# Three shared buffers between the copies of an accumulator and the transposes of u: who takes the third one, and three durations in the planner

## The chip, the cores and the metric

The kernel runs on one core of one Trainium2 chip. The metric is the device time of one execution in microseconds. The time before is 1109.25 us, the median of 3 runs (1109.18, 1109.25 and 1109.59 us). The execution that was profiled took 1109.22 us; its span, from the first to the last recorded instruction, is 1107.4 us, so 1.82 us of it lie around the span.

## The reference

Eight batches, each with a sequence of S = 3008 rows. An attention without softmax gates u, and an MLP mixer follows it, first over the tokens and then over the channels:

```python
def _attn_ref(u, v, z):                       # u, v: (8, 3008, 256), z: (8, 3008, 64)
    scores = (1.0 / S) * np.matmul(z, z.transpose(0, 2, 1))
    attn = np.maximum(scores, 0.0) ** 2
    return u * np.matmul(attn, v)

def _moe_ref(x, w_tok1, w_tok2, w_ch1, w_ch2):   # x is what the attention gave
    xt = x.transpose(0, 2, 1)
    h = np.maximum(xt @ w_tok1, 0.0) @ w_tok2     # 3008 -> 256 -> 3008
    u = x + h.transpose(0, 2, 1)
    h2 = np.maximum(u @ w_ch1, 0.0) @ w_ch2       # 256 -> 1536 -> 256
    return u + h2
```

## The kernel before, in words

**Tiling.** A batch `b` is cut into `NQ` = 6 blocks `q` of 512 rows (the last has 448). For each block the attention adds up `acc`, two accumulators `dh` = 0 and 1 of 128 columns of v each; each accumulator is held as two halves in a pair of PSUM banks, since the matmuls of `av_matmul` (L708) work on 64 rows at a time, two beside each other.

**From an accumulator to x.** When the last matmul of an accumulator is issued, `finish` (L820) plans three steps. `copy` (L833) has ACT copy one half to a buffer `cp` (L837); `add` (L842) has DVE add the other half to it (L843), after which the PSUM pair is free; `gate` (L854) has DVE multiply it with u (L865, and L870 for the 64 columns that are left in the last block) into `xT`, after which `cp` is free. After the second gate of a block, SP turns `xT` by a DMA transpose into `x_pair` (`turn_x`, L903), DVE makes differences of it (`x_sums`, L940), and from all six blocks `tok1` (L1075) begins the token mixer of the batch.

**The mixer.** `tok1` of six blocks gives `a_ps`. `collect_a` (L1095 on ACT, L1091 and L1106 on DVE) and `relu_a` (L1127 on ACT for one half, L1125 on DVE for the other) turn it into `a_f`; `tok2` (L1145) multiplies that and adds it to `xT` (L1154). From then on `xT` holds the mixer's u. `turn_u2` (L1176, DMA on SP at L1180) turns it into `u_sb`, which the output needs as the residual. The channel mixer is `ch1` (matmuls L1209 into `hp`, L1248 on ACT into `h2pre`) or, for some blocks, a form with fewer matmuls (`grouped_ch1`, L1340 into `gp`, with copies and activations at L1348, L1351, L1355 and L1359 on ACT). Then come seven `product`s per block (L1478, into `xb` and `zb`), from `h2pre` and from sums that DVE makes of it (`hsum`, L1414 to L1432). `collect` adds them, and `u_sb`, into `ro` (L1530, L1524); SP writes `ro` out (L1535).

**The three buffers.** `cp` and `u_sb` share one tag of three buffers (`tag="res", bufs=3`). A tile takes its buffer in the order in which the program is written down, and its first writer waits until what held the buffer is read.

**Who sets the order.** Nothing is ordered by hand and nothing at run time. While the program is built, a small simulation keeps a clock for PE (`pe[0]`), ACT, DVE and SP (`free`), and lists of waiting operations (`push`). `next_op` (L388) takes the operation that could start first: at the latest of its engine's time, its `ready`, and the first entry of its list `frees`, and only if its condition `room` holds. `push(engine, ready, busy, lat, fn)` states how long the engine is held and when the result is there. The work of PE is a list of `Piece`s with `needs`; `next_piece` (L1749) takes one whose needs are met at the clock's time, or within 0.05 us of it. `Sooner(done, us)` is a need that may be met `us` later than the piece's begin, because only a later matmul of the piece reads it. The instructions then stand in each engine's queue in the simulated order, and on the chip each queue works strictly in that order, waiting on semaphores where the data is not there.

**The stretches.** Attention and mixer alternate: when the last block of a batch is through its matmuls, `goal` is raised and only mixer pieces are taken: blocks q = 3, 4 and 5 of the batch before, then `tok1` and `tok2` of this batch, then its blocks 0 to 2. The transpose of u of blocks over `HALF` = 3 waits for that moment (L1168); that of block 3 is made at the end of the stretch before and holds one of the three buffers all through the attention.

**What the counters say before the change.** `copies[0]` counts copies between `copy` and `gate`, `live["us"]` the `u_sb` in use. A copy is planned only if `copies[0] + live["us"] < 3` (L850), a `turn_u2` if `live["us"] < 2` (L1167), whatever the copies hold. No time is kept at which a buffer comes free.

Of the kernel before, what the change touches and what calls it, by code (L numbers as in the profile page):

```python
# [69 lines left out]
def kernel(  # L70
# [298 lines left out]
    ROOM = {"at": 6, "fl": 11, "xT": 9, "h2": 6, "us": 2}  # L369
    at_free = [0.0] * ROOM["at"]  # L370
    fl_free = [0.0] * ROOM["fl"]
    ring = [(Done(0.0), i) for i in range(RING)]

    def first_acc(dh):
# [10 lines left out]
    def has_room(names):  # L385
        return names() if callable(names) else all(live[n] < ROOM[n] for n in names)
# [196 lines left out]
    def release(name, uses, t=0.0):  # L583
        uses[0] -= 1
        uses[1:] = [max([t] + uses[1:])]
        if not uses[0]:
            live[name] -= 1
            if name == "at":
                at_free.append(uses[1])
            if name == "fl":  # L590
                fl_free.append(uses[1])


    class Block:
# [225 lines left out]
    def finish(blk, dh, end):  # L820


        W, acc = blk.W, blk.acc[dh]
        summed = Done()
        guess[blk.home[dh]] = end + 1.7
        ring.append((summed, blk.home[dh]))

        def load(e):
            return max(free[e], end) + sum(op.busy for op in waiting[e])

        on_act = blk.b > 0 or load("act") + 0.46 < load("dve") + 0.67

        def copy(t):  # L833
            copies[0] += 1
            cp = sb.tile([P, QW], F32, tag="res", name="cp", bufs=3)
            if on_act:
                nc.scalar.copy(cp[:, :W], acc[:, 1, :W])  # L837
            else:
                nc.vector.tensor_copy(cp[:, :W], acc[:, 1, :W])
            push("dve", t, 0.66, 0.78, lambda t: add(cp, t), first=1, done=summed)  # L840

        def add(cp, t):  # L842
            nc.vector.tensor_add(cp[:, :W], acc[:, 0, :W], cp[:, :W])  # L843
            push("dve", t - 0.12, 0.58, 0.7, lambda t: gate(blk, dh, cp, t), first=1,
                 room=(lambda: (blk.b, blk.q) in uTs and has_room(("xT",))) if dh == 0
                 else lambda: (blk.b, blk.q) in xTs)

        engine, busy = ("act", 0.56 if blk.q == NQ - 1 else 0.46) if on_act else ("dve", 0.66)
        push(engine, end + 0.21, busy, busy + 0.15, copy, first=1,
             room=lambda: copies[0] + live["us"] < 3)  # L850

    gated, copies = [0], [0]

    def gate(blk, dh, acc, t):  # L854
        copies[0] -= not blk.whole
        b, q, W = blk.b, blk.q, blk.W
        uT = uTs[b, q]
        if dh == 0:
            xTs[b, q] = sb.tile([P, DT, QW], BF16, tag="xT", name="xT", bufs=ROOM["xT"])
            live["xT"] += 1  # L860
            if W < QW:
                nc.gpsimd.memset(xTs[b, q][:, :, W:], 0.0)
        xT = xTs[b, q]
        full, rest = W // P, W % P
        nc.vector.tensor_mul(  # L865
            xT[:, dh, :full * P].rearrange("p (t s) -> p t s", s=P),
            acc[:, :full * P].rearrange("p (t s) -> p t s", s=P),
            uT[:, :full, dh, :])
        if rest:
            nc.vector.tensor_mul(  # L870
                xT[:, dh, full * P:W], acc[:, full * P:W], uT[:, full, dh, :rest])
        if dh == DT - 1:
            if b == 0 and q > 1:
                release("fl", [1], t)
            gated[0] += 1
            push("sp", t, 1.25, 7.5 if q < NQ - 1 else 12.0, lambda t: turn_x(b, q, t),
                 first=1 if b == 0 or q >= NQ - 2 else -1,
                 room=x_room(b, q), frees=fl_free if b and q % 2 == 0 else ())
# [166 lines left out]
    def add_mixer(b):  # L1045
# [6 lines left out]
        def tok1(q, end):  # L1052
# [28 lines left out]
            if q == NQ - 1:  # L1081
                home = "fl" if b else "h2"

                def collect_a(t):
# [20 lines left out]
                    def one_high(t):  # L1105
                        nc.vector.tensor_add(f[:, 1, :], a_ps[:, 0, 3, :], f[:, 4, :])  # L1106
                        st["a"] = f[:, 6:8, :].rearrange("p k d -> p (k d)").bitcast(
                            BF16).rearrange("p (m d) -> p m d", m=2)
                        push("act", t, 0.3, 0.47, lambda t: relu_a(0, t), first=2,
                             done=a_done[0])  # L1110
                        push("dve", t - 0.16, 0.58, 0.72, both_high, first=2,
                             done=a_done[1])
# [26 lines left out]
        def tok2(q, end):  # L1139
# [9 lines left out]
            def add(t):  # L1149

                xT = xTs[b, q]
                n = full_tiles[q]
                to = xT[:, :, :n * P].rearrange("p h (t s) -> p h t s", t=n)
                nc.vector.tensor_add(  # L1154
                    to, to, h[:, :, :n * P].rearrange("p h (s t) -> p h t s", t=n))
                if n * P < W:
                    to = xT[:, :, n * P:W]
                    nc.vector.tensor_add(to, to, h[:, :, n * P:W])
                if W < QW and b % 2:

                    nc.gpsimd.tensor_copy(xT[:, :, W:], xT[:, :, W - TAIL:W])
                    t += 0.5
                u_done[q].t = t
                if ("want", q) in st:
                    st.pop(("want", q))(t)
                st["turned", q] = push("sp", t, 1.25, 5.5, lambda t: turn_u2(q, t), first=1,
                                       room=lambda: has_room(("us",)) and (  # L1167
                                           q <= HALF or goal[0] > (b, 1 + HALF)))  # L1168
            ring.append((push("dve", end + 0.21, 1.12, 1.25, add, first=2), slot))
            if q == NQ - 1:  # L1170
# [4 lines left out]

        def turn_u2(q, t):  # L1176
            live["us"] += 1
            turned_back[b] += 1
            us = sb.tile([P, DT, QW // P, P], BF16, tag="res", name="u_sb", bufs=3)
            nc.sync.dma_start_transpose(  # L1180
                out=us.rearrange("p h t d -> p (h t) d"),
                in_=xTs[b, q].rearrange("p h s -> p (h s)"))
            st["u", q] = us
            release("xT", xT_uses[q])
            for waits in st.pop(("waits", q), []):
                waits(t)
# [306 lines left out]
        def collect(q, k, end):  # L1493
# [24 lines left out]
            def add(t):  # L1518
# [15 lines left out]
                if not over[q]:  # L1534
# [1 line left out]
                        out=rows_of(out[b], q)[:, :2 * n, :], in_=st["res", q][:, :2 * n, :])  # L1536
                    free["sp"] = max(free["sp"], t) + 0.4
                    release(home_of(q), [1], t + 4.0)
                    release("us", us_uses[q])

            ready = end + 0.21
            done = taken[q, k]
# [41 lines left out]
        def ch2(q, half, i, end):  # L1584
# [23 lines left out]
            def residual(t):  # L1608
# [33 lines left out]
                        nc.sync.dma_start(out=to, in_=res[r, j, :])  # L1642
                free["sp"] = max(free["sp"], t) + 0.4
                if last:
                    release("us", us_uses[q])
            freed = Done()
            cost = 1.4 if both and b % 2 else 0.62
            with_u(q, end + 0.21, lambda at: push(
# [48 lines left out]

        def add_product(q, k):
            needs = {
                1: [Sooner(h2_done[q, c], 0.111 * c) for c in range(CHT // 2)] + w_done[2:],  # L1700
                2: [taken[q, 1]], 5: [mix_done], 6: [taken[q, 1]], 3: [taken[q, 5]], 7: [taken[q, 6]],
                4: [taken[q, 7]]}[k]
            if k == 2:
                needs = needs + [Read(taken[q, j]) for j in (6, 7)]
            kind = {5: 0, 7: 1, 6: 2, 4: 3}.get(k)
            if kind is not None:
                needs = needs + [Sooner(s_done[q, d, kind], 0.222 * d) for d in range(CHT // 4)]
            if q == NQ - 1 and k == 5 and b % 2 == 0:
                needs = needs + [tok1_over[b + 1]]
            cost = pairs_of(q) * (CHT // 2) * column_time(P)  # L1710
# [438 lines left out]
```

## Time and profile before

| | |
|---|---|
| median of 3 runs | 1109.25 us (1109.18 to 1109.59) |
| the profiled execution | 1109.22 us |
| its span | 1107.4 us |
| PE busy in the span | 1102.1 us, 11235 matmuls |
| DVE, ACT, POOL busy | 816.0, 694.9, 168.3 us |

PE is TensorE, DVE VectorE, ACT ScalarE, POOL GpSimd and SP SyncE. The chain of waits is the profile's account of what ended last, followed back step by step. In a timeline each row has its start and its length in us, the engine, the line of the kernel, the operation, what it writes and reads, the shape, and how many equal instructions are merged in it; in brackets stands how long the engine had nothing to do just before, and what ended that. Matmuls overlap in the pipeline, so the pace of PE is read from start to start: a 128x512 matmul takes 0.216 us that way, although its row shows a longer time. A wait inside a run of matmuls shows only there.

### The profile page before, as it was taken

Reading aid. Unit: us, or ns where it says so; the run is one execution under the profiler, and the core shown is the slowest. Engines: PE = TensorE matmul, PEld = TensorE weight load, DVE = VectorE, ACT = ScalarE, POOL = GpSimd, SP = SyncE. Lnnn points to the kernel's source line nnn. Section 1 sums busy time; section 2 is a strip of 40 time slices with the busy share of each in tenths; the row PEclk is TensorE's granted clock in tenths of the full one; section 3 lists DMA queues with packets and bytes.
Section 4 is the critical chain, followed back from the end, with each engine's and each line's share of the span. In section 5 each row is a group of like instructions: output and inputs, shape, how many; then the busy total and the mean of one; then the engine's idle time right before and its main releaser. Section 6 shows DMA issues by size and latency. Waiting matters only on the chain.

```text
span 1107.4 us, 27564 instructions
## 1 busy us (share of the span) xinstructions
PE 1102.1 (100%) x11235; PEld 699.6 (63%) x11235; DVE 816.0 (74%) x1727; ACT 694.9 (63%) x965; POOL 168.3 (15%) x386
## 2 busy tenths in 40 slices
PE   9999999999999999999999999999999999999998
PEld 3445575677557665576655865557655677556776
DVE  6889865877758867578765787667866778656785
ACT  8999565646855567556675467654766637753474
POOL 5320110321002110032100311003110030000100
PEclk9999999999999999999999999999999999999999
DMA  9999948797979979789697896976988769595213
GB/s 178 164 190 181 165 96 152 124 177 149 184 122 157 170 143 185 127 155 195 130 175 121 157 195 147 186 131 126 197 159 169 139 122 203 118 158 106 71 59 96
DMA packets 465728, 165.58 MB, mean 150 GB/s; under 512 B 433024, under 2 KB 448960, under 8 KB 465600
## 3 DMA queue, kind: packets, MB, share of 16 engines
q1 hardware_dynamic: 436208, 131.11, 59.0%
q0 software_dynamic: 28880, 32.32, 21.4%
q8 instruction: 88, 1.44, 0.6%
q14 instruction: 40, 0.33, 0.1%
q10 hardware_dynamic: 512, 0.38, 0.1%
HBM read 65.40 MB, written 24.64 MB: 81 GB/s over the span
## 4 chain that ended last, share of the span: by engine, by line
PE 97%; DVE 2%; ACT 1%; DMA 0%; issue 0%; POOL 0%; ACTq 0%
PE acc L708 41%; PE hp L1209 17%; PE xb L1478 13%; PE sc L481 6%; PE zb L1478 5%; PE gp L1340 4%; PE h_ps L1145 4%; PE a_ps L1075 3%; PE op L1599 2%; PE first_acc L625 1%; DVE at L527 1%; DMA v_sb<-in_v_dram 0%; ACT h2pre L1248 0%; PE wp L221 0%; DVE cp L843 0%; DVE shared_sb L985 0%
## 5 line engine op out<-in xcount | busy, mean ns | idle before, releaser
L708 PEld LDWEIGHTS <-v_sb 64*128 64x128 bf16 x4418 | 246.3, 94 | 211.5 <-issue 0.6
L708 PE MATMUL acc<-at,v_sb 64*128 64x512 bf16 (+1 forms) x2738 | 342.0, 375 | 0.0
L519 ACT ACTIVATE at<-sc 128x1024 bf16<-128x1024 f32 (+1 forms) x290 | 287.5, 1027 | 75.5 <-PE sc L481 70.0
L1248 ACT ACTIVATE h2pre<-hp 128x1024 bf16<-128x1024 f32 (+1 forms) x227 | 222.7, 1004 | 166.9 <-PE hp L1209 165.4
L527 DVE TENSOR_TENSOR at<-at 128x1024 bf16<-128x1024 bf16 (+1 forms) x290 | 197.0, 687 | 112.7 <-ACT at L519 107.6
L1209 PE MATMUL hp<-xT,w_ch_sb 128*128 128x512 bf16 (+1 forms) x936 | 227.2, 374 | 0.0
L708 PE MATMUL acc<-fl,v_sb 64*128 64x512 bf16 (+1 forms) x1680 | 192.9, 367 | 0.0
L1478 PEld LDWEIGHTS <-hsum 128*128 128x128 bf16 x2088 | 127.7, 98 | 12.1 <-issue 1.7
L481 PE MATMUL sc<-zT 64*128 64x512 bf16 (+1 forms) x732 | 133.2, 359 | 0.2 <-ACT zT L1977 0.2
L1209 PEld LDWEIGHTS <-w_ch_sb 128*128 128x128 bf16 x936 | 86.0, 98 | 72.2 <-issue 0.8
L1478 PEld LDWEIGHTS <-h2pre 128*128 128x128 bf16 x1566 | 96.6, 98 | 12.3 <-ACT h2pre L1248 0.4
L837 ACT COPY cp<-acc 128x512 f32<-128x512 f32 (+1 forms) x94 | 55.0, 585 | 76.8 <-PE acc L708 65.4
L843 DVE TENSOR_TENSOR cp<-acc,cp 128x512 f32<-128x512 f32 (+1 forms) x94 | 63.4, 674 | 47.7 <-ACT cp L837 47.3
L1414 DVE TENSOR_TENSOR hsum<-h2pre 128x1024 bf16<-128x1024 bf16 (+1 forms) x141 | 89.9, 649 | 10.5 <-ACT h2pre L1248 8.4
L1478 PE MATMUL xb<-w_ch_sb,h2pre 128*128 128x128 bf16 x1044 | 74.3, 219 | 0.2 <-ACT h2pre L1248 0.2
L140 POOL CAST mark<-at 128x1 f32<-128x1 bf16 x29 | 11.7, 403 | 411.0 <-DVE at L527 411.0
L1478 PE MATMUL xb<-shared_sb,hsum 128*128 128x128 bf16 x1044 | 73.7, 219 | 0.0
L507 ACT ACTIVATE at<-sc 128x512 bf16<-128x512 f32 (+3 forms) x152 | 56.0, 449 | 27.6 <-PE sc L481 23.3
L481 PEld LDWEIGHTS <-zT 64*128 64x128 bf16 x732 | 42.7, 94 | 41.4 <-issue 4.4
L865 DVE TENSOR_TENSOR xT<-cp,uT 128x512 bf16<-128x512 f32 (+1 forms) x94 | 62.9, 669 | 3.1
L1154 DVE TENSOR_TENSOR xT<-xT,h_ps 128x1024 bf16<-128x1024 bf16 (+1 forms) x48 | 55.6, 1172 | 3.1 <-PE h_ps L1145 2.8
L1432 DVE TENSOR_TENSOR hsum<-h2pre,hsum 128x512 bf16<-128x512 bf16 (+1 forms) x141 | 55.2, 401 | 2.3
(116 smaller groups left out, 1130.1 us busy)
## 6 DMA issues: line engine op xcount, KB each, us to landing
out_dram<-ro SPq DMA_DIRECT2D x40, 512.0 KB, 2.9
v_sb<-in_v_dram POOLq DMA_DIRECT2D x40, 256.0 KB, 4.6
ur<-in_u_dram POOLq DMA_DIRECT2D x40, 256.0 KB, 5.4
w_tok_sb<-in_moe_w_tok_dram POOLq DMA_DIRECT2D x10, 256.0 KB, 10.7
shared_sb<-in_z_dram POOLq DMA_DIRECT2D x35, 64.0 KB, 4.2
at<-at SPq DMA_TRANSPOSE x114, 2.4
out_dram<-ro SPq DMA_DIRECT2D x7, 256.0 KB, 3.7
fl<-at SPq DMA_TRANSPOSE x105, 4.5
```

The source lines that it names most:

```text
L481: nc.tensor.matmul(sc[:, r, c0:c1], zT[h, k:k + P], zT[h, m + c0:m + c1], start=True, stop=True)
L507: nc.scalar.activation(a3[:, i, c0:c1], sc[:, r, c0:c1], ACT.Relu, scale=inv_S)
L519: nc.scalar.activation(view, sv, ACT.Relu, scale=inv_S)
L527: nc.vector.tensor_mul(view, view, view)
L708: nc.tensor.matmul(o, vs[blk.b, g][rows, i, dh * P:(dh + 1) * P], rhs, start=(dh, h) not in blk.begun, stop=stop, skip_group_check=True)
L843: nc.vector.tensor_add(cp[:, :W], acc[:, 0, :W], cp[:, :W])
L865: nc.vector.tensor_mul(xT[:, dh, :full * P].rearrange("p (t s) -> p t s", s=P), acc[:, :full * P].rearrange("p (t s) -> p t s", s=P), uT[: ...
L1154: nc.vector.tensor_add(to, to, h[:, :, :n * P].rearrange("p h (s t) -> p h t s", t=n))
L1209: nc.tensor.matmul(hps[r % len(hps)][:, r, :W], w_ch1_sb[:, dc, cc * P:(cc + 1) * P], xT[:, dc, :W], start=(dc == 0), stop=(dc == DT - 1))
L1248: nc.scalar.activation(h2[:, :, :W], hp[:, :, :W], ACT.Relu)
L1414: nc.vector.tensor_sub(sums["s"][:, 0:2, :, :n * P], h[:, :, 1], h[:, 0])
L1478: nc.tensor.matmul(to[:, i * P:(i + 1) * P], lhs, weights[:, c2, :], start=(first_use and c2 == 0 and i == 0), stop=(c2 == CHT // 2 - 1), ...
```

## The change

Four things are edited.

1. A list `res_free` keeps the times at which the three `res` buffers come free, as the simulation has them. A copy and a `turn_u2` each take an entry; `gate` and the last use of `u_sb` each put one back. The copy is pushed with `frees=res_free`, so that it is planned no sooner than a buffer is free.
2. `turn_u2` also needs `copies[0] + live["us"] < 3`, and that `closing[0]` does not hold. `closing[0]` is set when an accumulator of the last block of a batch (from batch 1 on) is through its matmuls, and cleared when the copy of the second accumulator has its buffer.
3. `relu_a` of the first half on ACT is planned with 0.42 us held and 0.57 us to its result, instead of 0.3 and 0.47.
4. The allowances of `add_product` depend on how many pairs of 128 columns the block has (`pairs_of(q)`: 2, and 1 for the last block): 0.0556 us for each matmul instead of 0.111 us for each two, and 0.111 instead of 0.222. For the blocks with two they stay 0.111 and 0.222; for the last block they are halved.

```diff
     fl_free = [0.0] * ROOM["fl"]
+    res_free = [0.0] * 3
...
             if name == "fl":
                 fl_free.append(uses[1])
+            if name == "us":
+                res_free.append(uses[1])
...
         ring.append((summed, blk.home[dh]))
+        closing[0] = blk.b > 0 and blk.q == NQ - 1
...
         def copy(t):
             copies[0] += 1
+            res_free.pop(0)
+            if dh == DT - 1:
+                closing[0] = False
             cp = sb.tile([P, QW], F32, tag="res", name="cp", bufs=3)
...
         push(engine, end + 0.21, busy, busy + 0.15, copy, first=1,
-             room=lambda: copies[0] + live["us"] < 3)
-    gated, copies = [0], [0]
+             room=lambda: copies[0] + live["us"] < 3, frees=res_free)
+    gated, copies, closing = [0], [0], [False]
     def gate(blk, dh, acc, t):
-        copies[0] -= not blk.whole
+        if not blk.whole:
+            copies[0] -= 1
+            res_free.append(t)
...
-                        push("act", t, 0.3, 0.47, lambda t: relu_a(0, t), first=2,
+                        push("act", t, 0.42, 0.57, lambda t: relu_a(0, t), first=2,
                              done=a_done[0])
...
                 st["turned", q] = push("sp", t, 1.25, 5.5, lambda t: turn_u2(q, t), first=1,
                                        room=lambda: has_room(("us",)) and (
+                                           copies[0] + live["us"] < 3 and not closing[0]) and (
                                            q <= HALF or goal[0] > (b, 1 + HALF)))
...
         def turn_u2(q, t):
             live["us"] += 1
+            res_free.pop(0)
...
-                    release("us", us_uses[q])
+                    release("us", us_uses[q], t)
...
-                1: [Sooner(h2_done[q, c], 0.111 * c) for c in range(CHT // 2)] + w_done[2:],
+                1: [Sooner(h2_done[q, c], 0.0556 * pairs_of(q) * c) for c in range(CHT // 2)] + w_done[2:],
...
-                needs = needs + [Sooner(s_done[q, d, kind], 0.222 * d) for d in range(CHT // 4)]
+                needs = needs + [Sooner(s_done[q, d, kind], 0.111 * pairs_of(q) * d) for d in range(CHT // 4)]
```

More of the change, by code (lines that the diff above doesn't have):

```diff
@@ L1644, in residual @@
                 if last:
-                    release("us", us_uses[q])
+                    release("us", us_uses[q], t)
             freed = Done()
```

## Prediction

> **What bounds the kernel now.** First the page: span, busy times, and the shares of the chain that ended last.
>
> ```profile
> span 1107.4 us, 27564 instructions
> ...
> PE 1102.1 (100%) x11235; PEld 699.6 (63%) x11235; DVE 816.0 (74%) x1727; ACT 694.9 (63%) x965; POOL 168.3 (15%) x386
> ...
> PE 97%; DVE 2%; ACT 1%; DMA 0%; issue 0%; POOL 0%; ACTq 0%
> ```
>
> PE bounds the kernel, and the change removes none of its matmuls. It can only win or lose moments in which PE waits, and these are small: the 3% of the chain that is not PE's hold the start, the tail and every stall. Next, the table of waits, for the wait that the change names:
>
> ```profile
> ACT cp L837 <- DVE xT L870: 10.5, 6, 1.8
> ```
>
> Six times ACT stands before a copy until the gate of an earlier copy is through, 10.5 us in all. These are the ends of batches, L870 being the last block's second part. Timelines of SP, DVE and ACT there, batch 5:
>
> ```profile
> 742.76 1.30 SPq L1180 DMA_TRANSPOSE u_sb<-xT  x1
> ...
> 744.51 0.22 DVE L870 TENSOR_TENSOR xT<-cp,uT 128x64 bf16<-128x64 f32 x1
> ...
> 744.82 0.53 ACT L837 COPY cp<-acc 128x448 f32<-128x448 f32 x1 [1.80 <-DVE xT L870]
> ...
> 745.38 0.62 DVE L843 TENSOR_TENSOR cp<-acc,cp 128x448 f32<-128x448 f32 x1 [0.32 <-ACT cp L837]
> ...
> 746.80 1.23 SPq L903 DMA_TRANSPOSE x_pair<-xT  x1
> ```
>
> Block 3's u and the first copy hold two buffers; the transpose of block 4's u takes the third; so the second copy waits until the first is gated (744.73) and starts at 744.82. Its sum, which frees the PSUM pair, ends at 746.00. PE in the same stretch:
>
> ```profile
> 743.90 0.39 PE L1340 MATMUL gp<-xT,w_ch_sb 128*128 128x256 bf16 x2
> ...
> 745.01 1.03 PE L1209 MATMUL hp<-xT,w_ch_sb 128*128 128x512 bf16 x4
> 746.06 0.83 PE L1478 MATMUL zb<-shared_sb,hsum 128*128 128x128 bf16 x12
> ...
> 748.80 0.38 PE L1340 MATMUL gp<-xT,shared_sb 128*128 128x256 bf16 x2
> ```
>
> Attention is done at 743.90. From the four `hp` matmuls to the next run 1.05 us pass; the next run begins 0.06 us after that sum. Whether this is a loss is told by the last batch, where the same pieces run:
>
> ```profile
> 1012.72 0.39 PE L1340 MATMUL gp<-xT,w_ch_sb 128*128 128x256 bf16 x2
> ...
> 1013.31 0.53 ACT L837 COPY cp<-acc 128x448 f32<-128x448 f32 x1 [1.47 <-DVE xT L870]
> ...
> 1013.83 1.03 PE L1209 MATMUL hp<-xT,w_ch_sb 128*128 128x512 bf16 x4
> 1014.70 0.83 PE L1478 MATMUL zb<-shared_sb,hsum 128*128 128x128 bf16 x12
> 1015.37 0.38 PE L1340 MATMUL gp<-xT,w_ch_sb 128*128 128x256 bf16 x2
> ...
> 1017.34 0.38 PE L1340 MATMUL gp<-xT,shared_sb 128*128 128x256 bf16 x2
> ```
>
> Here the second copy starts 0.59 us after the end of attention (1013.31 - 1012.72), there 0.92 (744.82 - 743.90). The four `hp` take 0.87 us, and from `hp` to the last `gp` row 3.51 us pass, against 3.79 in batch 5. So 0.33 us of a sooner copy removed the whole wait, 0.28 us. The pace is read here too: 0.87 / 4 = 0.217 us for a 128x512 matmul, 0.67 / 12 = 0.056 us for a 128x128 one.
>
> **The change part by part.**
>
> *Buffers, later batches.* The first and the last of the five such stretches (batches 2 to 6):
>
> ```profile
> 337.70 1.03 PE L1209 MATMUL hp<-xT,w_ch_sb 128*128 128x512 bf16 x4
> ...
> 341.49 0.38 PE L1340 MATMUL gp<-xT,shared_sb 128*128 128x256 bf16 x2
> ...
> 880.17 1.03 PE L1209 MATMUL hp<-xT,w_ch_sb 128*128 128x512 bf16 x4
> ...
> 883.96 0.38 PE L1340 MATMUL gp<-xT,shared_sb 128*128 128x256 bf16 x2
> ```
>
> Both take 3.79 us. With the change the transpose of u may not be planned before the second copy has its buffer, so that copy finds one free and needs only its accumulator: some 0.15 to 0.2 us after attention's end in place of 0.92 (an estimate: the first copy, gate and sum all follow their data by under 0.2 us here). That is sooner than in the last batch, where the wait was gone already. Gain 5 x 0.28 = **1.40 us**. What is late next: `hsum` on DVE and the release of `gp` by ACT, both in time in the last batch at a copy 0.59 us in; so I take all of it. The last batch itself gains nothing, its PE not waiting.
>
> *Buffers, batch 1.* ACT, then PE:
>
> ```profile
> 199.29 0.53 ACT L837 COPY cp<-acc 128x448 f32<-128x448 f32 x1 [0.66 <-PE hp L1209]
> 199.72 3.78 ACT L1248 ACTIVATE h2pre<-hp 128x1024 bf16<-128x1024 f32 x4
> ...
> 201.72 0.72 PE L1478 MATMUL xb<-w_ch_sb,h2pre 128*128 128x128 bf16 x10
> 202.64 0.28 PE L1478 MATMUL xb<-w_ch_sb,h2pre 128*128 128x128 bf16 x2 [0.19 <-ACT h2pre L1248]
> ```
>
> ACT is idle for 0.66 us before the second copy, then evacuates four `hp` without a break, and PE is held inside a product: 202.64 - 201.72 - 10 x 0.056 = **0.36 us**. The profile names `hp` as the releaser, which that copy does not read; I take it to be the buffer again. Copy and evacuations move up by about 0.4 to 0.66 us, more than the stall; I take 0.36.
>
> *The transpose of u that waits.* It comes after the first gate (744.73) instead of at 742.76, 2.0 us later. Its rows, and its first reader (block 4's first sum):
>
> ```profile
> L1180 SPq DMA_TRANSPOSE u_sb<-xT x48: 1233/1476/3512, 130.0 to 1089.9; - x48
> ...
> DMA to landing us min/median/max: 2.7/4.2/8.5
> ...
> 757.15 0.41 DVE L1530 TENSOR_TENSOR ro<-zb,u_sb 128x256 f32<-128x256 f32 x1
> ```
>
> 744.73 + 8.5, the slowest landing, is 753.2: 3.9 us of cover, cost nothing. Behind it in SP's queue stands the last block's `x_pair` (746.80, after the second gate). At the usual 1.2 to 1.5 us SP is free again by 746.2, and the second gate comes sooner as well. If the cover is gone: second rival.
>
> *`frees` on copies.* Only one u holds a buffer through the attention, and two are left for copies that are gated one after the other; I see no place where a copy would be planned later for it. Cost nothing; if I am wrong, ACT takes another operation first and a pair comes free some 0.6 us later, which PE's other pieces cover or not.
>
> *Allowances for the last block.* In every second batch its first product waits at its end for the sixth `h2pre`; first and last of four:
>
> ```profile
> 221.89 0.62 PE L1478 MATMUL xb<-w_ch_sb,h2pre 128*128 128x128 bf16 x6
> 222.34 0.28 PE L1075 MATMUL a_ps<-x_pair,w_tok_sb 128*128 128x128 bf16 x2
> ...
> 1033.19 0.62 PE L1478 MATMUL xb<-w_ch_sb,h2pre 128*128 128x128 bf16 x6
> 1033.65 0.28 PE L1075 MATMUL a_ps<-x_pair,w_tok_sb 128*128 128x128 bf16 x2
> ```
>
> 0.45 and 0.46 us for 6 x 0.056 = 0.34: 0.12 us lost, 4 x 0.12 = 0.46 us. Planned true, the product is ready 5 x 0.0556 = 0.28 us later, and a `tok1` piece can go ahead of it. That shifts all later pieces around `tok1`, which no row prices: between the full 0.46 and as much lost again. I take half, **0.23**.
>
> *`relu_a`.* Its rows, then the PE runs between which the first `tok2` waits for it, first and last of three (batches 1, 5 and 7):
>
> ```profile
> L1127 ACT ACTIVATE a_f<-a_f x8: 408/416/417, 118.3 to 1039.5; 128x256 bf16<-128x256 f32 x8
> ...
> 228.12 0.50 PE L1478 MATMUL zb<-shared_sb,h2pre 128*128 128x128 bf16 x6
> 228.65 1.04 PE L1145 MATMUL h_ps<-w_tok_sb,a_f 128*128 128x512 bf16 x4
> ...
> 1039.43 0.50 PE L1478 MATMUL zb<-shared_sb,h2pre 128*128 128x128 bf16 x6
> 1039.95 1.04 PE L1145 MATMUL h_ps<-w_tok_sb,a_f 128*128 128x512 bf16 x4
> ```
>
> 0.42 us is what it takes; 0.3 was planned. PE loses 0.53 - 0.34 = 0.19 us, three times 0.57. But the plan is put right by only 0.10 us, about half of the lateness, so another piece may still not be chosen. Between 0.57 and a like loss; I take a third, **0.19**.
>
> The sum: 1.40 + 0.36 + 0.23 + 0.19 = 2.18 us. A new order brings stalls of its own; I allow two of the usual size here, 0.12 us each, 0.24. That leaves 1.94 us: the profiled execution's 1109.22 becomes 1107.28. It lies 0.03 under the median of the runs, so the forecast is **1107.3 us**.
>
> The Trainium skill speaks against a gain: Perfetto Trace Analysis, section Identifying Performance Opportunities, says that improving a kernel generally means improving its most contended engine. By that, an idle ACT at 63% is worth nothing and the time stays 1109.2. [...]
>
> **The rivals.** *All of it comes:* both re-set durations remove their whole stalls and nothing is given back: 1.40 + 0.36 + 0.46 + 0.57 = 2.79, **1106.4 us**. For it: a `tok1` piece ahead of the product leaves one more product to cover `relu_a`. Against it: no batch of this trace has an order of pieces that leaves no stall of 0.1 us or more.
>
> *The stall changes its name:* the PSUM pair is free earlier, but PE then waits as long for another thing, or the re-planned stretch puts its loss elsewhere. ACT has been idle through 37% of the span without harm. **1109.2 us**. Against it: the last batch, where a sooner copy did remove the wait. That the buffer is not the cause, and the transpose would have stood behind the copy anyway, gives the same time.
>
> *x comes late:* the held transpose of u lands ahead of the last block's `x_pair` in SP's queue and takes 3.5 us there, its longest; the token mixer needs that block, so `tok1` slips by as much.
>
> ```profile
> 762.34 0.28 PE L1075 MATMUL a_ps<-x_pair,w_tok_sb 128*128 128x128 bf16 x2
> ```
>
> What PE could do meanwhile are the last block's seven products, 7 x 6 x 0.056 = 2.35 us. From a slip of 2.35 us on PE stands idle: 1.15 us in each of six stretches, 6.9 us, less the 1.94 gained: **1114 us**. Against it: `x_pair` starts at 746.80 and `tok1` at 762.34, and a median transpose leaves SP free in time.
>
> **How the numbers follow.** The forecast has 0.45 (its own range 1106.6 to 1108.2), all of it 0.25, the changed name 0.18, late x and other losses of a new order 0.12. A measurement of this kernel tells about 0.2%, 2.2 us, from no change: below 1107.0 is faster, above 1111.5 slower. Faster has the 0.25 and a third of the forecast's, 0.40; same 0.48; slower 0.12. The range goes from 1106.0 (all of it, and 0.4 us of other stalls) to 1109.8 (the changed name, and what a few stalls add); late x stays out.
>
> **What the changed profile would show.** Right: no wait of a copy for L870 at the batch ends, the second copy within 0.3 us of attention's end, 3.5 us from `hp` to the last `gp` row in batches 2 to 6, u's transpose after the second copy's start. Wrong: the same stretches still at 3.8 us; `tok1` starting later after `x_pair` than 15.5 us; or new stalls over 1 us in the attention stretches, which I take to keep their order.

## The result, and the profile after

The changed kernel takes 1107.45 us (median of 21 runs, 1106.81 to 1110.48), the kernel before 1109.83 us beside it (21 runs, 1109.17 to 1111.77): ratio 0.9979 [0.9972, 0.9986], 2.4 us or 0.21% faster. The forecast was 1107.3 us. The profiled execution took 1107.47 us. From its page, span, busy times and the chain that ended last:

```profile
span 1105.6 us, 27508 instructions
...
PE 1097.4 (99%) x11172; PEld 701.7 (63%) x11235; DVE 816.0 (74%) x1727; ACT 696.4 (63%) x965; POOL 165.3 (15%) x386
...
PE 96%; DVE 2%; DMA 1%; issue 1%; ACT 0%; DVEq 0%; ACTq 0%
```

No work went away. PE's matmuls seem fewer (11172 against 11235), but PEld, DVE, ACT and POOL have the counts of before: 63 records are missing from this trace, and with them some busy time. So all times below are read from start to start (and an x3 stands for four `hp`). The table of waits (us in total, times, longest) no longer has an entry of a copy that waits for a gate; in its place stands

```profile
ACT cp L845 <- DVE cp L851: 4.9, 5, 1.0
```

Of the same place as in the prediction, the end of batch 5's attention (the lines have moved: L845 was L837, L851 was L843, L880 was L870, L913 was L903, L1085 was L1075, L1155 was L1145, L1192 was L1180, L1221 was L1209, L1260 was L1248, L1352 was L1340, L1490 was L1478), the timeline of all engines in order of time:

```profile
742.87 0.39 PE L1352 MATMUL gp<-xT,w_ch_sb 128*128 128x256 bf16 x2
...
742.98 0.53 ACT L845 COPY cp<-acc 128x448 f32<-128x448 f32 x1 [0.98 <-DVE cp L851]
...
743.74 1.23 SPq L1192 DMA_TRANSPOSE u_sb<-xT  x1
...
743.96 0.62 DVE L851 TENSOR_TENSOR cp<-acc,cp 128x448 f32<-128x448 f32 x1
743.99 1.03 PE L1221 MATMUL hp<-xT,w_ch_sb 128*128 128x512 bf16 x3
...
744.85 0.83 PE L1490 MATMUL zb<-shared_sb,hsum 128*128 128x128 bf16 x12
...
745.37 1.23 SPq L913 DMA_TRANSPOSE x_pair<-xT  x1
...
747.49 0.38 PE L1352 MATMUL gp<-xT,shared_sb 128*128 128x256 bf16 x2
```

The second copy starts 0.11 us after the end of attention (742.98 - 742.87; 0.92 before) and the transpose of u after it. The sum that frees the PSUM pair ends at 744.58, and the `zb` run, due at 743.99 + 0.87 = 744.86, starts at 744.85: PE no longer waits there, and the sum has 0.27 us to spare. The profile names DVE's sum as what the copy waits for. But the row of the accumulator's last matmul ends only at 742.94 (the next matmul starts at 742.87), and the copy starts 0.04 us after that end, as the copies do that the profile puts down to their accumulator. So it now follows its data.

From `hp` to the last `gp` row 3.50 us pass; before they were 3.79. Two waits of PE make up the difference. The first, 0.18 us (1.05 - 0.87 before), stood before `zb` and is the one that the prediction's rows show. The second, 0.10 us, stood before the last `gp` row, which started 2.74 us after `zb` (748.80 - 746.06) and now starts 2.64 us after it (747.49 - 744.85). Its rows before the change, PE and ACT:

```profile
747.84 1.03 PE L1209 MATMUL hp<-xT,w_ch_sb 128*128 128x512 bf16 x4
...
748.18 0.57 ACT L1348 COPY gp<-gp 128x512 f32<-128x512 f32 x1
```

PE was due at 747.84 + 0.87 = 748.71. ACT, which had worked without a pause since the late copy, was through with the copy inside `gp` at 748.75, and the `gp` row followed at 748.80.

In batch 1, ACT and PE:

```profile
198.79 0.53 ACT L845 COPY cp<-acc 128x448 f32<-128x448 f32 x1
199.60 3.77 ACT L1260 ACTIVATE h2pre<-hp 128x1024 bf16<-128x1024 f32 x4 [0.28 <-PE hp L1221]
...
201.99 0.83 PE L1490 MATMUL xb<-w_ch_sb,h2pre 128*128 128x128 bf16 x12
202.66 1.03 PE L1221 MATMUL hp<-xT,w_ch_sb 128*128 128x512 bf16 x4
```

Copy and evacuations are earlier, and the twelve matmuls run through in 0.67 us (202.66 - 201.99): the 0.36 us are gone.

Where the rest came from is read from a ledger. The start of the first copy of each batch is a mark that all kernels have (batch 0 is counted into column 1, from its first copy on); the table shows by how much the time from one batch's mark to the next (in batch 7, to the end of the span) differs from before, in us. Kernels of the experiments stand beside the change.

| kernel | 1 | 2 | 3 | 4 | 5 | 6 | 7 | sum |
|---|---|---|---|---|---|---|---|---|
| the change | -0.48 | -0.43 | -0.41 | +0.03 | -0.40 | -0.29 | -0.13 | -2.11 |
| the change, again | -0.50 | -0.43 | -0.41 | -0.31 | -0.40 | -0.29 | -0.12 | -2.46 |
| buffers alone (e1) | -0.36 | -0.29 | -0.28 | -0.35 | -0.29 | -0.28 | -0.01 | -1.86 |
| `closing` alone (e6) | -0.36 | -0.29 | -0.28 | -0.35 | -0.29 | -0.29 | -0.01 | -1.87 |
| allowances alone (e7) | -0.11 | +0.01 | -0.13 | -0.03 | -0.11 | 0.00 | -0.11 | -0.48 |
| `closing` and allowances (e12) | -0.50 | -0.29 | -0.41 | -0.31 | -0.41 | -0.29 | -0.13 | -2.34 |

The span of the profiled execution fell by 1.8 us only, since its load phase took 0.27 us longer, before anything that the change touches (first mark at 35.41 us, before 35.15).

Batch 4 gives nothing in this execution: a new stall there. Its rows on SP, PE and DVE, then those of the same kernel in another execution:

```profile
658.84 0.53 SPq L1547 DMA_DIRECT2D out_dram<-ro  x1
...
664.02 1.89 PE L1221 MATMUL hp<-xT,w_ch_sb 128*128 128x512 bf16 x8
664.75 0.69 DVE L1426 TENSOR_TENSOR hsum<-h2pre 128x1024 bf16<-128x1024 bf16 x1 [1.03 <-DMA out_dram<-ro]
665.36 0.68 DVE L1536 TENSOR_TENSOR ro<-xb,u_sb 128x512 f32<-128x512 f32 x1
666.09 0.38 PE L1352 MATMUL gp<-xT,w_ch_sb 128*128 128x256 bf16 x2 [0.18 <-DVE ro L1536]
```

```profile
658.24 0.53 SPq L1547 DMA_DIRECT2D out_dram<-ro  x1
...
664.00 1.89 PE L1221 MATMUL hp<-xT,w_ch_sb 128*128 128x512 bf16 x8
664.41 0.68 DVE L1536 TENSOR_TENSOR ro<-xb,u_sb 128x512 f32<-128x512 f32 x1
665.72 0.38 PE L1352 MATMUL gp<-xT,w_ch_sb 128*128 128x256 bf16 x2
```

An output was issued 0.60 us later and landed 5.8 us after its issue, at about 664.6; in the other execution it took 5.5 us to land. DVE stood before `hsum` for that landing, its `ro` behind it came 0.95 us later (665.36 against 664.41), and that `ro` frees the bank for `gp`. PE lost 2.07 - 8 x 0.217 = 0.33 us. In the other execution `hp` to `gp` took 1.72 us, with no loss.

### The profile page after: what moved, and what is told of

The parts are those of the page before. It is cut to its first block, busy times and chain, and to the rows that moved or that the text cites. A ratio compares the mean times of both kernels' runs of the same rounds, so it can differ in the third digit from the quotient of the medians.

```text
span 1105.6 us, 27508 instructions
## 1 busy us (share of the span) xinstructions
PE 1097.4 (99%) x11172; PEld 701.7 (63%) x11235; DVE 816.0 (74%) x1727; ACT 696.4 (63%) x965; POOL 165.3 (15%) x386
## 4 chain that ended last, share of the span: by engine, by line
PE 96%; DVE 2%; DMA 1%; issue 1%; ACT 0%; DVEq 0%; ACTq 0%
PE acc L711 41%; PE hp L1221 17%; PE xb L1490 13%; PE sc L482 6%; PE zb L1490 5%; PE h_ps L1155 4%; PE gp L1352 4%; PE a_ps L1085 3%; PE op L1611 2%; PE first_acc L628 1%; DVE at L528 1%; DMA out_dram<-ro 1%; PE wp L221 0%; DVE hsum L1426 0%; DVE cp L851 0%
## 5 line engine op out<-in xcount | busy, mean ns | idle before, releaser
L1260 ACT ACTIVATE h2pre<-hp 128x1024 bf16<-128x1024 f32 (+1 forms) x227 | 222.6, 1003 | 168.0 <-PE hp L1221 163.4
L1221 PE MATMUL hp<-xT,w_ch_sb 128*128 128x512 bf16 (+1 forms) x883 | 224.3, 373 | 2.7
L1490 PEld LDWEIGHTS <-hsum 128*128 128x128 bf16 x2088 | 127.8, 98 | 10.9 <-DVE hsum L1426 0.3
L1221 PEld LDWEIGHTS <-w_ch_sb 128*128 128x128 bf16 x936 | 86.2, 98 | 72.0 <-issue 0.8
L1490 PEld LDWEIGHTS <-h2pre 128*128 128x128 bf16 x1566 | 96.5, 98 | 11.4
L845 ACT COPY cp<-acc 128x512 f32<-128x512 f32 (+1 forms) x94 | 55.0, 585 | 75.5 <-PE acc L711 70.4
L851 DVE TENSOR_TENSOR cp<-acc,cp 128x512 f32<-128x512 f32 (+1 forms) x94 | 63.4, 675 | 49.6 <-ACT cp L845 49.3
L1490 PE MATMUL xb<-w_ch_sb,h2pre 128*128 128x128 bf16 x1044 | 73.6, 219 | 0.1
L1490 PE MATMUL xb<-shared_sb,hsum 128*128 128x128 bf16 x1044 | 73.6, 219 | 0.0
```

The source lines that it names most:

```text
L1221: nc.tensor.matmul(hps[r % len(hps)][:, r, :W], w_ch1_sb[:, dc, cc * P:(cc + 1) * P], xT[:, dc, :W], start=(dc == 0), stop=(dc == DT - 1))
L1260: nc.scalar.activation(h2[:, :, :W], hp[:, :, :W], ACT.Relu)
L1490: nc.tensor.matmul(to[:, i * P:(i + 1) * P], lhs, weights[:, c2, :], start=(first_use and c2 == 0 and i == 0), stop=(c2 == CHT // 2 - 1), ...
```

## The experiments

The theory is that of the prediction: the second copy waits for a buffer, the copy's lateness holds the PSUM pair, the pair holds PE, and the change takes the buffer out of it. Rivals: the planner's times (`res_free`) or another order of work bring the gain; the durations do; the late transpose of u is paid for at x.

**The buffers alone.** The change, with the three durations of before:

```diff
-                        push("act", t, 0.42, 0.57, lambda t: relu_a(0, t), first=2,
+                        push("act", t, 0.3, 0.47, lambda t: relu_a(0, t), first=2,
...
-                1: [Sooner(h2_done[q, c], 0.0556 * pairs_of(q) * c) for c in range(CHT // 2)] + w_done[2:],
+                1: [Sooner(h2_done[q, c], 0.111 * c) for c in range(CHT // 2)] + w_done[2:],
...
-                needs = needs + [Sooner(s_done[q, d, kind], 0.111 * pairs_of(q) * d) for d in range(CHT // 4)]
+                needs = needs + [Sooner(s_done[q, d, kind], 0.222 * d) for d in range(CHT // 4)]
```

> Only the buffer part of the change; the three planned durations are those of before. Theory (the second copy of a batch's last block waits for a buffer, and PE behind it): in batches 2 to 6 from the four hp matmuls to the third gp group 3.51 us in place of 3.79, in batch 1 no stall of 0.36 us inside the product, together 1.76 us: a ratio of 0.9984 to the kernel before. The 0.12 us waits of the last block's first product in batches 1, 3, 5 and 7 stay. Rival (the gain comes from the re-set durations or from the luck of a new order): the wait of the copy goes, but PE's 3.79 us stay or come back elsewhere, 0 to 0.5 us gained, ratio 0.9995 or more.

1108.20 us (12 runs, 1107.46 to 1112.57) against 1109.67; ratio 0.9987 [0.9978, 0.9995]; 1.86 us in the ledger. On every engine and in SP's queue, its instructions stand in the same order as those of the kernel before: only which of the three buffers an operation takes is different. So this gain is waits alone, and no other order. The run also put the rival of late x to a small test, by accident. Batch 5, SP and PE:

```profile
743.49 2.60 SPq L1192 DMA_TRANSPOSE u_sb<-xT  x1
746.19 1.25 SPq L913 DMA_TRANSPOSE x_pair<-xT  x1
...
760.78 0.28 PE L1085 MATMUL a_ps<-x_pair,w_tok_sb 128*128 128x128 bf16 x2
```

The held transpose happened to take 2.60 us in place of 1.23, and `x_pair` started 3.57 us after the end of attention (742.62 here), later than before (2.90). `tok1` began 18.16 us after that end, exactly as in the change (761.03 - 742.87). So a slip of 0.67 us costs nothing; that rival has PE idle only from 2.35 us on, which this does not test.

**The durations alone.** The kernel before, with the three new durations (the diff above, the other way round).

> Only the re-set durations (relu_a and the last block's allowances); the buffers are planned as before. Theory: the second copy still waits 1.80 us at five batch ends, 3.79 us from hp to gp; the 0.12 us waits go in batches 1, 3, 5 and 7, 0.46 us, and nothing for relu_a in batches 1, 5 and 7, where the profile of the change still shows 0.19 us: ratio 0.9996. Rival: most of the 2.1 us, ratio 0.9985 or less.

1109.13 us (12 runs, 1108.66 to 1112.71); ratio 0.9997 [0.9988, 1.0005]: not told from no change. All waits of the copies stay. In the ledger it gains 0.55 us in columns 2 to 7. Column 1 can't be read, since the profiled execution holds one stall of 4 us near 110 us, ahead of all that the durations touch; so its span says nothing either.

**`closing` alone.** The kernel before, with one flag: no transpose of u is planned from the end of the last block's attention until its second copy has its buffer.

```diff
+        closing[0] = blk.b > 0 and blk.q == NQ - 1
...
+            if dh == DT - 1:
+                closing[0] = False
...
-                                       room=lambda: has_room(("us",)) and (
+                                       room=lambda: has_room(("us",)) and not closing[0] and (
```

> The kernel before with nothing but the closing condition on the transpose of u; no times of free buffers, no count for the transpose, durations of before. Theory: it is only who takes the third buffer, so this gives all of the buffer part: copies wait no more for a gate at batch ends, 3.51 us from hp to gp in batches 2 to 6, 1.4 to 1.8 us gained, ratio 0.9984 to 0.9987. Rival (the plan needs the times too): the transpose, planned at once behind the copy, holds SP up while it waits for the first gate, x_pair of the last block starts later than in the change, and less than 1 us is gained.

1107.99 us (10 runs, 1107.13 to 1108.67); ratio 0.9979 [0.9970, 0.9988]. Ledger and orders are those of e1. The times in `res_free` and the count of buffers add nothing once the flag is there.

**Without `closing`.** The change, with count and times but without the flag:

```diff
-                                           copies[0] + live["us"] < 3 and not closing[0]) and (
+                                           copies[0] + live["us"] < 3) and (
```

> The change without the closing condition; the count over copies and u, the times of free buffers and the durations stay. Theory: between the two copies of the last block only one copy and one u hold buffers, so the transpose takes the third as before, the second copy waits 1.8 us again, and only the durations' 0.46 us are left, ratio 0.9996. Rival (count and times are what does it): like the whole change, ratio 0.998.

Both expectations missed: 1122.57 us (4 runs, 1117.70 to 1127.04), ratio 1.0116 [1.0086, 1.0145]. At each of six batch ends (batches 2 to 7) PE waits 1.5 to 3.2 us, 11.9 us in all. Batch 3, all engines:

```profile
475.16 1.03 PE L1221 MATMUL hp<-xT,w_ch_sb 128*128 128x512 bf16 x3
...
476.06 0.55 ACT L845 COPY cp<-acc 128x448 f32<-128x448 f32 x1
...
477.99 0.42 DVE L950 TENSOR_TENSOR d_pair<-x_pair 128x512 bf16<-128x512 bf16 x1 [1.43 <-DMA x_pair<-xT]
...
478.54 0.62 DVE L851 TENSOR_TENSOR cp<-acc,cp 128x448 f32<-128x448 f32 x1
...
479.21 1.44 PE L1490 MATMUL zb<-shared_sb,hsum 128*128 128x128 bf16 x12 [3.02 <-DVE cp L851]
```

The planner now knows that the buffer comes late. On ACT it queues three other copies ahead of the second copy, which starts at 476.06, 2.01 us after the end of attention (474.05). On DVE it queues differences of `x_pair` ahead of the sum; here one of them waits 1.43 us for its transpose, and the sum behind it starts at 478.54, 1.93 us after its copy was done (476.61).

**The count alone.** As the last, and without the times on the copies:

```diff
-             room=lambda: copies[0] + live["us"] < 3, frees=res_free)
+             room=lambda: copies[0] + live["us"] < 3)
```

> The change without the closing condition and without the times of free buffers on the copy; the count over copies and u stays for the transpose, and the re-set durations. Theory (the 13 us that the change loses without the closing condition come from the times: the copy, planned true behind the gate of the first, lets DVE's differences of x be queued ahead of the copy's sum, and these wait for a late DMA): the plan holds the copy sooner again, the waits are those of before, 3.8 us from hp to gp, ratio 0.9995. Rival (the count on the transpose loses it): ratio 1.01 as without closing alone.

1109.54 us (10 runs, 1108.74 to 1113.27); ratio 1.0000 [0.9991, 1.0010]. Its orders are those of the durations alone, and its table of waits has the old entry again:

```profile
ACT cp L845 <- DVE xT L880: 11.1, 7, 1.8
```

So the 13 us of the run without `closing` came from the times: the plan was truer about the buffer, and by it put work that can wait ahead of the copy and the sum on which PE waits.

**A second copy that takes longer.** The change, with the last block's second copy made twice (one line less than shown), then three times. ACT is held some 0.56 us longer for each.

```diff
                 nc.scalar.copy(cp[:, :W], acc[:, 1, :W])
+                if blk.b > 0 and blk.q == NQ - 1 and dh == DT - 1:
+                    nc.scalar.copy(cp[:, :W], acc[:, 1, :W])
+                    nc.scalar.copy(cp[:, :W], acc[:, 1, :W])
```

> The change, with the second copy of each batch's last block made twice (from batch 1 on; the same values into the same buffer), which the plan does not know of: that copy's result comes 0.45 us later, all queues in the order of the change. Theory (the release of the PSUM pair by this copy and its sum, and ACT's queue behind the copy, decide PE's stretch): from the four hp matmuls to the third gp group some 3.75 to 3.85 us again in batches 2 to 6 in place of 3.51, so 1.2 to 1.7 us of the gain are lost. Rival (PE is bound by something else there): 3.5 us stay.

Twice: 1107.43 us (1 run; before 1109.60), hardly a loss. DVE and PE, batch 5 (L853 is the sum, L851 in the change; L1354 is L1352):

```profile
743.93 1.03 PE L1223 MATMUL hp<-xT,w_ch_sb 128*128 128x512 bf16 x4
744.06 0.62 DVE L853 TENSOR_TENSOR cp<-acc,cp 128x448 f32<-128x448 f32 x1
...
747.48 0.38 PE L1354 MATMUL gp<-xT,shared_sb 128*128 128x256 bf16 x2
```

The stretch takes 3.55 us, where I had expected 3.75 to 3.85. In the change the sum doesn't start when the copy is done (743.51) but at 743.96, when DVE is through with a `hsum`, 1.09 us after the end of attention. Here the longer copy is done at 744.03, and the sum starts 1.25 us after that end (744.06 - 742.81). It moves by 0.16 us only, less than the 0.27 it has to spare, and `zb` does not wait. (The expectation that follows says 0.1, which is 744.06 - 743.96 without the difference of the two ends.) The 0.05 us come before the last `gp` row, by ACT. In batch 1, where PE follows ACT's `h2pre`, 0.15 us are lost.

> The change, with the second copy of each batch's last block made three times (the plan does not know of it). Made twice it moved the sum that frees the PSUM pair by only 0.1 us, because DVE was not free sooner anyway: the sum ended 1.87 us after attention's end, and the zb product, due 1.98 us after it, did not wait. Theory: one more copy puts the sum at about 2.4 us, and zb waits some 0.5 us: 4.0 us from the four hp matmuls to the third gp group in batches 2 to 6 in place of 3.5. Rival (zb does not wait for this sum at all): 3.5 to 3.6 us stay.

Three times: 1111.66 us (1 run; before 1109.89). PE, ACT and DVE, batch 5 (L848 is the third copy, L854 the sum):

```profile
746.46 1.03 PE L1224 MATMUL hp<-xT,w_ch_sb 128*128 128x512 bf16 x3
746.59 0.53 ACT L848 COPY cp<-acc 128x448 f32<-128x448 f32 x1
...
747.15 0.62 DVE L854 TENSOR_TENSOR cp<-acc,cp 128x448 f32<-128x448 f32 x1 [0.64 <-ACT cp L848]
...
747.83 0.83 PE L1493 MATMUL zb<-shared_sb,hsum 128*128 128x128 bf16 x12 [0.34 <-DVE cp L854]
```

Now PE waits 747.83 - 746.46 - 0.87 = 0.50 us, until 0.06 us after the sum (747.15 + 0.62): the same gap as before the change. This shows the chain from copy to sum to PSUM pair to PE, and its slack. From `hp` to the last `gp` row 4.11 us pass, where 4.0 were expected: the other 0.11 us stand before that row, which starts at 750.57, again 0.05 us after ACT's copy inside `gp` ends (750.52). So a late copy holds PE in two ways, through the sum and the PSUM pair and through ACT's queue behind it.

**The allowances alone.** The kernel before, with the two `Sooner` lines of the change.

> The kernel before with the last block's allowances alone re-set (relu_a planned as before). Theory: the 0.12 us waits of the first product go in batches 1, 3, 5 and 7 (0.46 us), and since the tok1 piece ahead of it leaves the relu_a waits as they were, this is all. Rival: the allowances do nothing alone, and the 0.7 us that the two durations gained together come from relu_a.

1109.36 us (1 run; before 1109.60). The ledger gives 0.48 us, 0.46 of it in batches 1, 3, 5 and 7, where they were due; the waits before `tok2` stay.

**A later `relu_a`.** The change, with a still later completion in the plan:

```diff
-                        push("act", t, 0.42, 0.57, lambda t: relu_a(0, t), first=2,
+                        push("act", t, 0.42, 0.87, lambda t: relu_a(0, t), first=2,
```

> The change, with relu_a's result planned 0.87 us after its start instead of 0.57. Theory (0.10 us was too little to move another piece in front of tok2): in batches 1, 5 and 7 a product goes ahead of the first tok2, its wait of 0.19 us goes, 0.57 us gained over the change, ratio 0.9974 to the kernel before. Rival (no other piece is ready there): the same order and the same 0.19 us, or a longer wait by what is planned more.

1108.71 us (11 runs, 1108.28 to 1109.06); ratio 0.9987 [0.9978, 0.9996], 0.9 us behind the change by the two ratios. PE, batch 5:

```profile
769.78 0.50 PE L1490 MATMUL zb<-shared_sb,h2pre 128*128 128x128 bf16 x6
770.65 0.49 PE L1490 MATMUL xb<-w_ch_sb,hsum 128*128 128x128 bf16 x6 [0.38 <-DVE ro L1542]
```

A product now goes ahead of `tok2`, as was meant, and waits 770.65 - 769.78 - 0.33 = 0.54 us itself, for a bank that DVE frees late (the `ro` in brackets). Batches 1 and 7 lose the same 0.54 us, and batches 4 and 6 now lose 0.30 at this place. The 0.19 us before `tok2` were cheaper.

**Outputs that land later in the plan.** The change, with the release of the output's buffers planned 2 us later, for batch 4's stall:

```diff
-                    release(home_of(q), [1], t + 4.0)
+                    release(home_of(q), [1], t + 6.0)
```

> The change, with the buffer of an output tile planned free 6.0 us after its DMA is issued instead of 4.0. Theory for the 0.34 us stall that the change's profile shows in batch 4 (a sum stands 1.03 us before a buffer whose output DMA has not landed, and a product's bank comes free late behind it): the stall goes, 0.3 us gained over the change, ratio 0.9976, if the later planning moves nothing else. Rival: the order changes in all batches and loses as much or more.

1107.61 us (11 runs, 1107.23 to 1108.65); ratio 0.9983 [0.9974, 0.9992]. Batch 4's stall is gone, as it is in another execution of the change itself (below), so this one proves little. The new order waits some 0.25 us before `tok2` in four batches, where the change waits 0.19 in three. Batch 5:

```profile
769.72 0.50 PE L1490 MATMUL xb<-w_ch_sb,hsum 128*128 128x128 bf16 x6
770.31 1.90 PE L1155 MATMUL h_ps<-w_tok_sb,a_f 128*128 128x512 bf16 x8
```

0.59 us for 0.33 of work: 0.25 lost. No gain in the sum.

**`closing` and the allowances**, on the kernel before: no times, no count, `relu_a` as it was.

> The kernel before with the closing condition and the last block's allowances, without the times of free buffers, without the count for the transpose and with relu_a planned as before. Theory (these two lines are the change): 1.86 + 0.46 us gained, less what batch 4 loses by its new order, ratio 0.9979 like the whole change; batch 2 keeps its 0.14 us wait for relu_a. Rival: what is left out carries some of it, ratio 0.9985 or more.

1107.32 us (9 runs, 1106.82 to 1109.02; before 1109.89); ratio 0.9973 [0.9963, 0.9982].

**The change again**, beside it:

> The change itself once more, profiled again. Theory (the 0.34 us stall in batch 4, at the third mixer block, is a matter of when an output's DMA lands, not of the order, since the kernel with closing and allowances has the same order there without it): the stall is there with another size, between 0 and 0.35 us, and everything else keeps its place within 0.05 us: 3.5 us stretches, 0.19 us before tok2 in batches 1, 5 and 7. Rival (the order makes it): 0.34 us again.

1107.32 us (10 runs, 1106.84 to 1109.38; before 1109.91); ratio 0.9980 [0.9970, 0.9989]. No stall in batch 4, and every engine has the same order in both executions, so the order does not make it. Its ledger is in the table. The runs of this kernel and of `closing` and the allowances can't be told apart. The ledger has the change 0.12 us ahead, all of it in batch 2, which without the new duration of `relu_a` keeps its wait (-0.29 for -0.43). So a flag and two lines do all but this of what the whole change does. A fourth buffer, which would part copies and u altogether, was not tried.

## Why the prediction was right, and where it was not

**Buffers: right, by its mechanism.** 1.40 + 0.36 = 1.76 us were forecast, 1.86 came with this part alone. 0.28 us in each of five batches and 0.36 in batch 1 went as worked out; 0.01 in batch 7, as said. The rest is some 0.07 us in batch 4. What the step took for one wait of 0.28 us were two, 0.18 through the PSUM pair and 0.10 through ACT; both went with the same copy. That I could take all of it is shown by the slack of the sum, 0.27 us, and by the two longer copies: one more copy costs 0.05 us in such a stretch, two more cost 0.61. That it is the buffer in batch 1 too was a guess, and right: before the change the second copy started at 199.29, 0.08 us after the gate of the first (198.99 + 0.22), as in batch 5 (744.73 and 744.82).

**Allowances: mis-sized.** I took half of 0.46 us, since no row priced the shift of later pieces. The whole came, 0.48 alone. After the change the first product of batch 1 takes no wait:

```profile
222.57 0.50 PE L1490 MATMUL xb<-w_ch_sb,h2pre 128*128 128x128 bf16 x6
222.91 0.28 PE L1085 MATMUL a_ps<-x_pair,w_tok_sb 128*128 128x128 bf16 x2
```

0.34 us, as 6 x 0.056 asks. A `tok1` piece took its place, and nothing was given back.

**`relu_a`: the size near, the place wrong.** I took 0.19 of the 0.57 us that `tok2` waits in batches 1, 5 and 7. All three waits stay; batch 1 after the change:

```profile
227.90 0.50 PE L1490 MATMUL zb<-shared_sb,h2pre 128*128 128x128 bf16 x6
228.43 1.04 PE L1155 MATMUL h_ps<-w_tok_sb,a_f 128*128 128x512 bf16 x3
```

0.53 us, as before. What went is a wait that I had not listed, in batch 2. Before, then after:

```profile
363.45 0.50 PE L1478 MATMUL zb<-shared_sb,h2pre 128*128 128x128 bf16 x6
363.93 1.04 PE L1145 MATMUL h_ps<-w_tok_sb,a_f 128*128 128x512 bf16 x4
```

```profile
362.95 0.50 PE L1490 MATMUL zb<-shared_sb,h2pre 128*128 128x128 bf16 x6
363.29 0.50 PE L1490 MATMUL xb<-w_ch_sb,hsum 128*128 128x128 bf16 x6
363.62 1.03 PE L1155 MATMUL h_ps<-w_tok_sb,a_f 128*128 128x512 bf16 x3
```

There 0.14 us went, since a product was put between. That the plan was put right by half of the lateness only, as the step said, was the reason that three waits stayed. The later completion shows that more of it would not have paid.

**New stalls: 0.24 us taken, 0.34 found** in the profiled execution and none in the other. By the ledger, buffers 1.86, allowances 0.48 and batch 2's 0.14 make 2.48, against 2.46 measured without that stall. The forecast's gain was 1.94. It had 0.10 too little for the buffers, 0.25 too little for the allowances and had taken off 0.24 for stalls that did not come there, against 0.05 too much for `relu_a`; these errors add up to some 0.5 us and do not cancel. That the time of 1107.45 us lies only 0.15 from the forecast is partly luck: beside the change the kernel before took 1109.83 us, 0.58 more than the 1109.25 from which the forecast set out, so the measured gain is 2.4 us and not 1.9.

**The times cost nothing: right only because of `closing`.** I saw no place where they would plan a copy later. Without the flag there are six, and 13 us. The step's reason ("copies that are gated one after the other") left out the transpose of u, which can still take the third buffer there.

**The checks.** No copy waits for the gate; 0.11 us for 0.3; 3.50 us; u's transpose after the second copy's start, 2.0 us later against the end of attention (0.87 after it in place of 1.14 ahead): all as written. No stall of 1 us came into an attention stretch; no column of the ledger grew by more than 0.03. One sign was badly chosen. `tok1` starts 15.66 us after `x_pair` (761.03 - 745.37), over my 15.5. But before the change it is 15.54 (762.34 - 746.80), over it already, and `x_pair` is itself earlier now, 2.50 us after the end of attention in place of 2.90. Against that end `tok1` is sooner by the gain, 18.16 for 18.44 us.

**The rivals.** The stall did not change its name, and x was not late. "All of it" asked for 2.79 us; 2.46 came, since `tok2` still waits in three batches.

I had read the Trainium skill, Perfetto Trace Analysis, section Identifying Performance Opportunities, as speaking against a gain. That was too narrow: for the most contended engine the same section asks for the gaps on that engine and for what it waits for in them. PE is that engine, 100% busy before and with no less work after. Its gaps of 0.10 to 0.36 us gave the 0.21%, 1.86 us of it through who takes a buffer among ACT, DVE and SP. The section's sign that buffers may be too few, the same gap repeated on the engine that should be saturated, is here on PE too, 0.28 us in each of five stretches; an order among three buffers was enough.

## What to carry to other kernels

A busy share of 100% still holds waits of 0.1 to 0.4 us: compare equal stretches of several batches from start to start, and the one that is shorter tells what the others lose. Where something not urgent can take the last buffer of a shared ring just ahead of something urgent, one condition on the planner, for that moment alone, is enough. Planning that buffer's late release truly instead was far worse here, since the urgent copy then went behind all that the plan had ready before it.

## What the runs showed of the hardware

TensorE's clock fell during a wait in the run without `closing`. Three stretches of its table of windows (length, busy times and counts, granted clock, DMA share, GB/s):

```profile
477.00:479.00 2.00, 0.00 (x0) 0.00 (x0) 1.01 (x3) 0.54 (x1) 0.00 (x0) 0.95 1.26 268
479.00:481.00 2.00, 1.79 (x15) 1.66 (x15) 1.70 (x6) 0.00 (x0) 0.00 (x0) 0.50 0.14 30
481.00:484.00 3.00, 3.00 (x29) 2.35 (x28) 2.14 (x10) 1.69 (x3) 0.63 (x2) 0.80 0.78 175
```

PE waited from 476.03 (475.16 + 0.87) to 479.21. The 0.95 of the first stretch puts the fall at 478.8, 2.8 us into the wait, and the 0.80 of the last puts its end at 482.2: half clock for 3.4 us. That cost about 1.4 us more (12 matmuls of `zb` took 480.44 - 479.21 = 1.23 us for 0.67). With the 11.9 us of waits this makes 13.3; the two spans are 13.2 us apart (1118.8 and 1105.6).

The length of the wait alone does not tell whether the clock falls. In the durations alone PE waited 2.2 us near 110 us, and the clock was 0.50 for 3.4 us from 111.6 on. After a wait of 2.19 us in batch 4 of the run without `closing`, and one of 2.6 us near 102 us in the count alone, it stayed at 1.00. The Trainium skill, TensorE: Matmul & The Clock Gate, Part 1, has half clock after at least one idle window of about 3.4 us, and says that this window runs freely. The trace agrees with the half clock, which lasted 3.4 us both times. A wait as long as such a window was not needed: 2.2 us were enough once.

The output of batch 4's stall took 5.8 us to land, and 5.5 us where nothing stalled; the median of such outputs is 2.9. So its issue, 0.60 us later, did more than its landing. Single stalls of 4 to 5 us, each in one profiled execution, stood between 100 and 112 us in the durations alone and in the count alone. In both ACT waits for the landing of `fl<-at`, a DMA transpose of the attention (2.9 us in the first, 2.8, 1.5 and 1.3 in the second); why it landed late stays open.
